# A two-layer decode kernel on one core: one transpose per K unit, a q projection with stationary weights, and a new plan of loads

## The chip, the cores and the metric

One core of a Trainium2 chip. The metric is device time in microseconds for one execution of the whole program; lower is better.

## The reference

Two rounds of attention and feed-forward with the same weights and the same K and V caches. Batch 4, one query token, 32 query heads over 8 K/V heads, 8192 cached positions, head size 128, model width 512, feed-forward width 1792, everything in bf16.

```python
def _A_ref(x, k_cache, v_cache, wq, wo):
    q = (x @ wq).reshape(B, Sq, Hq, Dh).transpose(0, 2, 1, 3)
    k = jnp.repeat(k_cache, rep, axis=1); v = jnp.repeat(v_cache, rep, axis=1)
    scores = jnp.einsum("bhqd,bhkd->bhqk", q, k) * (Dh ** -0.5)
    o = jnp.einsum("bhqk,bhkd->bhqd", _softmax(scores), v)
    return o.transpose(0, 2, 1, 3).reshape(B, Sq, Hq * Dh) @ wo

x = x + _A_ref(_layernorm(x), A_k_cache, A_v_cache, A_wq, A_wo)   # layer 0
x = x + _B_ref(_layernorm(x), B_w_gate, B_w_up, B_w_down)
x = x + _A_ref(_layernorm(x), A_k_cache, A_v_cache, A_wq, A_wo)   # layer 1, same caches
x = x + _B_ref(_layernorm(x), B_w_gate, B_w_up, B_w_down)
```

K and V are 64 one-MiB units each (named by batch, group of heads and half of the cache). Both layers read all of them; what stays in SBUF between the layers need not be read twice.

## The kernel before

All loads go through one queue, which before's profile shows busy for 97.7% of 16 DMA engines' time; a load counts as landed when its semaphore has been raised 16 times:

```python
def dma(self, engname, out_ap, in_ap, sem, reads=(), writes=()):
    self._wait(engname, self._need(reads, writes))
    ins = self.eng[engname].dma_start(out_ap, in_ap)
    ...
    ins.then_inc(sem, 16)
```

A scheduler in Python, with a planned duration for each step, fixes the order of work on each engine; `ORDER` fixes the order of the loads, and with it which units are kept. At run time each engine works strictly in that order: in after, TensorE waits 4.07 us for one unit while the next in its order has lain there since 620.64 us (shown below).

```python
ORDER = ("c320 K c321 ... b231 b350 b330 b331 b361 ")   # ... cut; K: the next K unit, a/b/c: V units, w: weights
NSLOT = 11
KM = (0, 0, 0, 0)            # K units kept of each batch
```

A K unit is transposed in place in two halves, and its scores are 32 matmuls of 512 columns (4 slices of the head x 4 blocks of rows x 2 halves), so that they need both halves early on:

```python
for h in range(2 if ld is not None else 0):
    def t(h=h):
        ap, key = unit_ap(u, h)
        v = ap.bitcast(mybir.dt.uint32)
        op("dve", lambda e: e.transpose(v, v), reads=[key], writes=[key])
    tr.append(PL.add("dve", 1.23, t, [ld], prio))
...
for es_ in range(NES):
    for a in range(4):
        for h in range(2):
            op("pe", lambda e: e.matmul(ps[...], lhsT=qpad[rows, qbuf, es_, g, :], rhs=ap[h][rows, :, es_ // 2, :, es_ % 2], ...))
```

Between the layers, batch by batch, lies what I call a crossing: the rest of layer 0 for that batch, the feed-forward block, and the q projection of layer 1, in two halves of 16 heads with the activations stationary and `wq` moving, which leaves the result in rows (128x512 in the trace) that VectorE transposes in 0.73 us:

```python
def q_rows(hf, deps, tag):
    ...
    for kt in range(KT):
        for n in range(4):
            op("pe", lambda e: e.matmul(ps[32 * n:32 * n + B, bk * BW:(bk + 1) * BW],
                                        lhsT=xnT[:, kt * B:(kt + 1) * B], rhs=w[:, :, 32 * n:32 * (n + 1)], ...))
```

Of the kernel before, what the change touches and what calls it, by code (L numbers as in the profile page):

```python
# [115 lines left out]
class Plan:  # L116
# [140 lines left out]
    def emit(self):  # L257
        for s in sorted(self.steps + self.loads, key=lambda s: (s.start, s.prio[0])):
            s.fn()


ORDER = ("c320 K c321 c041 c240 a061 wg0 K a071 c241 wo2 K x wq K c201 a051 a021 K c131 K c130 a031 c311 K K "
         "c110 K c111 K K c120 c121 c051 c040 K K K K K wo0 K a020 K a030 wg1 K a060 wo3 K c261 a070 K c050 K "
         "K K K c301 c260 K K K K K K a050 K a040 a041 a000 a001 wo1 a011 a010 c340 wd1 wu0 c341 wu1 wd0 a140 "
         "a141 a160 a171 a170 a161 K K K K K c200 K K K K K K c300 K K K K K a100 a101 a150 a151 K K a130 K "
         "a120 a121 K K K K K a111 K K K K K a110 K K a131 b000 b001 K b021 b030 b020 b070 b031 b071 b010 "
         "b011 K K K a210 K K K K K K K K K K K K K a270 a271 K a220 a250 a221 K a211 K K a230 a240 K K K "
         "b100 c060 K a200 a241 K c061 K a251 a231 K K K K a260 a201 a261 b150 K K b101 b161 b151 b170 b160 "
         "b171 b140 b141 K a310 a350 K K K K K K K K K K a351 K K K K K a370 a361 a360 a371 a330 a301 a340 "
         "a320 a341 a311 a300 a331 a321 b210 b211 b270 b271 b230 K K K K K K K K K K K K K K K K b221 b251 "  # L270
         "b250 b220 b371 b370 b351 b310 b360 b231 b350 b330 b331 b361 ")
NSLOT = 11
NP = 2
NQB = 1
LATE = (6, )
KM = (0, 0, 0, 0)
TAILSPLIT = True


def bass_interleave_layers__gqa_block_cached__swiglu_ffn__decode_kernel(  # L280
# [12 lines left out]
    B, _, D = A_x.shape  # L293
    _, G, S, Dh = A_k_cache.shape
# [19 lines left out]
    with ExitStack() as es:  # L314
# [107 lines left out]
        def pbk(key):  # L422
            return PL.bank[key]
# [46 lines left out]
                           reads=[f"wq{kt}", "xnT"], writes=[f"pb{bk}"], sig=(kt == KT - 1 and h == heads[-1]))  # L470
            return PL.add("pe", 0.029 * KT * len(heads), mm, deps, CHAIN, take=tag, n=2 * KT * len(heads))

        def q_rows(hf, deps, tag):
            nh = Hq // 2

            def mm():
                bk = pbk(tag)
                for kt in range(KT):
                    w = wq_sb[:, kt, hf * nh * Dh:(hf + 1) * nh * Dh].rearrange("p (h d) -> p h d", d=Dh)
                    for n in range(4):  # L480
                        op("pe", lambda e: e.matmul(ps[32 * n:32 * n + B, bk * BW:(bk + 1) * BW],  # L481
                                                    lhsT=xnT[:, kt * B:(kt + 1) * B],
                                                    rhs=w[:, :, 32 * n:32 * (n + 1)],
                                                    start=(kt == 0), stop=(kt == KT - 1), tile_position=(0, 32 * n)),
                           reads=[f"wq{kt}", "xnT"], writes=[f"pb{bk}"], sig=(kt == KT - 1 and n == 3))
            return PL.add("pe", 1.3, mm, deps, CHAIN, take=tag, n=2 * 4 * KT)

        def q_spread(src, n, key, deps, tag):
            def mm():
                bk = pbk(tag)  # L490
# [46 lines left out]
        def q_half(b, hf, mm_tag, deps, prior):  # L537
            nh = Hq // 2
            k = kpos[(1, b)] % NQB

            def scl():
                bk = pbk(mm_tag)
                blk = bank(bk).bitcast(mybir.dt.uint32)
                op("dve", lambda e: e.transpose(blk, blk), reads=[f"pb{bk}"], writes=[f"pb{bk}"])  # L544
                src = ps[:, bass.ds(bk * BW + b, nh, step=32)]
                op("dve", lambda e: e.tensor_scalar(qT2[:, hf * nh:(hf + 1) * nh], src, qscale[:, b:b + 1], None,  # L546
                                                    op0=ALU.mult),
                   reads=[f"pb{bk}", "qscale"], writes=[f"qT2_{hf}"])
            s1 = PL.add("dve", 0.98, scl, deps, CHAIN, free=mm_tag)
            tag = f"qs{b}_{hf}"  # L550
            sp = q_spread(qT2[:, hf * nh:(hf + 1) * nh], nh, f"qT2_{hf}", [s1], tag)

            def cp():
                bk = pbk(tag)
                got = ps[:, bk * BW:bk * BW + NES * nh].rearrange("p (s g j) -> p s g j", s=NES, j=REP)
                op("dve", lambda e: e.tensor_copy(q_diag(k, hf * G // 2, G // 2), got),
                   reads=[f"pb{bk}"], writes=[f"qpad{k}_{hf}"])
            return PL.add("dve", 0.21, cp, [sp, prior], CHAIN, free=tag)
# [36 lines left out]
        def k_pair(u, ld, prio, prev):  # L595
            _, l, b, g, cp = u
            qbuf = kpos[(l, b)] % NQB
            tr = []
            seq = [x[3:] for x in k_units(l, b)]
            first, last = [[c for c in seq if c[1] == cp][i] == (g, cp) for i in (0, -1)]  # L600
            for h in range(2 if ld is not None else 0):
                def t(h=h):
                    ap, key = unit_ap(u, h)
                    v = ap.bitcast(mybir.dt.uint32)
                    op("dve", lambda e: e.transpose(v, v), reads=[key], writes=[key])  # L605
                tr.append(PL.add("dve", 1.23, t, [ld], prio))
            qd = q_ready[(l, b)][2 * g // G]

            def qk():
                kt = [unit_ap(u, h) for h in range(2)]  # L610
                ap = [k[0].rearrange("p (t e j s) -> p t e j s", e=2, j=32, s=2) for k in kt]
                for es_ in range(NES):
                    for a in range(4):
                        rows = slice(32 * a, 32 * (a + 1))
                        for h in range(2):
                            c = 2 * cp + h
                            op("pe", lambda e: e.matmul(ps[32 * c:32 * (c + 1), a * BW:(a + 1) * BW],  # L617
                                                        lhsT=qpad[rows, qbuf, es_, g, :],
                                                        rhs=ap[h][rows, :, es_ // 2, :, es_ % 2],
                                                        start=(first and es_ == 0),  # L620
                                                        stop=(last and es_ == NES - 1),
                                                        tile_position=(32 * a, 32 * c), skip_group_check=True),
                               reads=[f"qpad{qbuf}_{2 * g // G}", kt[h][1]], writes=[f"pb{a}"],
                               sig=(es_ == NES - 1 and a == 3 and h == 1))
            st = PL.add("pe", 1.95, qk, tr + [qd, prev] + (scores_free[0] or []), prio, n=64)
            if u not in kept_k:
                st.slot_of = home[u]
            return st
# [249 lines left out]
        def chain(b, deps, prior):  # L878
# [6 lines left out]
            mm = None  # L885
            for hf in range(2):
                tag = f"q{b}_{hf}"
                mm = q_rows(hf, [cen, mm], tag)
                out_.append(q_half(b, hf, tag, [mm, qs], prior))
            if b == B - 1:  # L890
                mm.gives = KT
# [185 lines left out]
```

## Time and profile before

| | before |
|---|---|
| median of 4 runs | 640.68 us (639.79 to 641.46) |
| profiled span | 638.1 us |
| K and V loads | 231 of 1 MiB, 256.14 MB with the weights |
| one-MiB load in an undisturbed stretch | 2.487 us from landing to landing, 421 GB/s |
| last load landed | 627.12 us |

In the profile, the busy line, the queue's share and the chain that ended last say that transfers set the time; the prediction below shows them.

```profile
q8 instruction: 65, 1.06, 0.7%
...
L605 DVE STREAM_TRANSPOSE pool<-pool 128x1024 uint32<-128x1024 uint32 x240 | 284.2, 1222 | 72.8 <-DMA pool<-in_A_k_cache_dram 66.6
```

Columns of the first: packets, MB, share of 16 engines' time. 65 packets, each of 16,384 bytes in the trace; 8,273 matmuls and as many weight loads are 16,546 instructions, 255 to a packet. I read each as a page of TensorE's instructions. The second: 240 transposes of half a unit, mean 1222 ns.

The end of the stream in TensorE's timeline (start, duration, what, and in brackets the idle time before it and what ended it):

```profile
624.68 1.05 PE L758 MATMUL ps<-pool,pp 128*32 128x256 bf16 x16 [0.84 <-DMA pool<-in_A_v_cache_dram]
625.93 0.59 PE L743 MATMUL ps<-pp,pool 128*128 128x4 bf16 x16 [0.20 <-DMA pool<-in_A_v_cache_dram]
627.16 0.59 PE L743 MATMUL ps<-pp,pool 128*128 128x4 bf16 x16 [0.65 <-DMA pool<-in_A_v_cache_dram]
627.61 0.99 PE L721 MATMUL ps<-oT,wo_sb 128*128 128x4 bf16 x32
```

Each load is used the moment it lands, and 0.5 us after the last one the output projection starts.

### The profile page before, as it was taken

The numbers are of one execution on the slowest core, as the hardware profiler recorded it, in microseconds if no ns is written. First come the engines' busy times: TensorE is split into PE (matmuls) and PEld (weight loads), VectorE is DVE, ScalarE is ACT, GpSimd is POOL, SyncE is SP. The second block draws the span as 40 slices with busy tenths as digits, with TensorE's granted clock in tenths as the row PEclk, the third lists the DMA queues.
The fourth block names the chain that finished last, engine by engine and source line by source line (L and its number), as shares of the span: only waits on it lengthen the run. The fifth ranks groups of instructions, "written<-read, shape, count | busy, mean of one in ns | idle before, by whom it ended". The sixth has DMA issues, their size and how long they took to land.

```text
span 638.1 us, 17970 instructions
## 1 busy us (share of the span) xinstructions
PE 420.7 (66%) x8273; PEld 198.9 (31%) x8273; DVE 428.0 (67%) x752; ACT 40.2 (6%) x106; POOL 1.8 (0%) x8
## 2 busy tenths in 40 slices
PE   0176566756677776677677576768577766876576
PEld 0131133224332242135322232225332244522255
DVE  3248868863379886766689857467588762599632
ACT  0000100011000020000100100000200020000200
POOL 1000000000000000000000000000000000000000
PEclk9997668685556667676676777575766675578685
DMA  8999999999989999999999999999999999999992
GB/s 349 416 421 420 408 404 421 418 410 390 412 347 417 423 419 419 422 418 408 407 398 421 422 417 420 422 419 412 416 405 420 416 420 421 393 420 420 421 416 85
DMA packets 41124, 257.29 MB, mean 403 GB/s; under 512 B 3924, under 2 KB 9816, under 8 KB 11096
## 3 DMA queue, kind: packets, MB, share of 16 engines
q1 hardware_dynamic: 41048, 256.14, 97.7%
q8 instruction: 65, 1.06, 0.7%
q14 instruction: 11, 0.09, 0.0%
HBM read 256.12 MB, written 0.00 MB: 401 GB/s over the span
## 4 chain that ended last, share of the span: by engine, by line
DMA 66%; DVE 15%; PE 15%; SPq 2%; issue 2%; ACT 0%
DMA pool<-in_A_k_cache_dram 37%; DMA pool<-in_A_v_cache_dram 24%; DVE pool L605 10%; PE ps L617 5%; PE ps L758 4%; DMA wo_sb<-in_A_wo_dram 3%; DMA wq_sb<-in_A_k_cache_dram 2%; SPq L92 2%; PE ps L481 1%; PE ps L804 1%; DVE negm L636 1%; PE ps L676 1%; DVE ps L544 1%; DVE ps L785 1%; DVE wq_sb L605 1%
## 5 line engine op out<-in xcount | busy, mean ns | idle before, releaser
L605 DVE STREAM_TRANSPOSE pool<-pool 128x1024 uint32<-128x1024 uint32 x240 | 284.2, 1222 | 72.8 <-DMA pool<-in_A_k_cache_dram 66.6
L617 PE MATMUL ps<-pool,qpad 32*32 32x512 bf16 x3840 | 222.0, 542 | 75.7 <-DVE pool L605 75.1
L758 PE MATMUL ps<-pool,pp 128*32 128x256 bf16 x1952 | 99.8, 358 | 61.1 <-DMA pool<-in_A_v_cache_dram 44.9
L617 PEld LDWEIGHTS ps<-pool,qpad 32*32 32x32 bf16 x3840 | 63.9, 109 | 210.6 <-DVE pool L605 149.9
L758 PEld LDWEIGHTS ps<-pool,pp 128*32 128x32 bf16 x1952 | 56.1, 120 | 101.6 <-DMA pool<-in_A_v_cache_dram 62.6
L785 DVE STREAM_TRANSPOSE ps<-ps 128x256 f32<-128x256 f32 x63 | 28.8, 458 | 65.6 <-PE ps L758 65.6
L640 ACT ACTIVATE pp<-ps,negm 128x512 bf16<-128x512 f32 x32 | 21.5, 685 | 305.5 <-DVE negm L636 289.0
L721 PE MATMUL ps<-oT,wo_sb 128*128 128x4 bf16 x640 | 22.6, 166 | 15.5 <-DVE oT L789 7.5
L636 DVE TENSOR_REDUCE negm<-ps 128x1 f32<-128x512 f32 x32 | 19.9, 683 | 16.5 <-PE ps L617 16.5
L721 PEld LDWEIGHTS ps<-oT,wo_sb 128*128 128x128 bf16 x640 | 20.0, 102 | 27.3 <-DVE oT L789 13.6
L676 PE MATMUL ps<-ident,pp 128*128 128x128 bf16 x128 | 14.2, 285 | 9.1 <-DVE pp L665 8.3
L605 DVE STREAM_TRANSPOSE wq_sb<-wq_sb 128x1024 uint32<-128x1024 uint32 x16 | 18.6, 1212 | 0.5 <-DMA wq_sb<-in_A_k_cache_dram 0.2
L452 ACT ACTIVATE lnv<-var,eps_sb 128x4 f32<-128x4 f32 x10 | 3.0, 297 | 234.6 <-DVE var L447 234.6
L617 PE MATMUL ps<-wq_sb,qpad 32*32 32x512 bf16 x256 | 12.6, 409 | 7.1 <-DVE wq_sb L605 6.9
L676 PEld LDWEIGHTS ps<-ident,pp 128*128 128x128 bf16 x128 | 11.3, 131 | 15.9 <-DVE pp L665 11.0
L481 PE MATMUL ps<-wq_sb,xnT 128*4 128x512 bf16 x128 | 13.9, 589 | 1.9 <-DVE qT L546 1.4
L965 PE MATMUL ps<-ident,pp 4*128 4x4 bf16 x4 | 0.3, 167 | 21.0 <-DMA pp<-in_A_x_dram 21.0
L787 DVE TENSOR_REDUCE osum<-ps 128x4 f32<-128x32 f32 x63 | 12.1, 192 | 2.1
L789 DVE TENSOR_TENSOR oT<-osum,invL 128x4 bf16<-128x4 f32 x63 | 10.6, 169 | 2.1
L544 DVE STREAM_TRANSPOSE ps<-ps 128x512 uint32<-128x512 uint32 x8 | 5.8, 725 | 7.8 <-PE ps L481 7.8
L685 ACT ACTIVATE pp<-ps 128x1024 bf16<-128x1024 bf16 x8 | 8.2, 1023 | 35.3 <-PE ps L676 35.3
L804 PE MATMUL ps<-xnT,wu_sb 128*128 128x4 bf16 x280 | 8.6, 166 | 2.0 <-DVE gs L824 1.5
(69 smaller groups left out, 160.0 us busy)
## 6 DMA issues: line engine op xcount, KB each, us to landing
pool<-in_A_k_cache_dram SPq DMA_DIRECT2D x120, 1024.0 KB, 10.5
pool<-in_A_v_cache_dram SPq DMA_DIRECT2D x98, 1024.0 KB, 11.8
wq_sb<-in_A_k_cache_dram SPq DMA_DIRECT2D x8, 1024.0 KB, 14.4
wo_sb<-in_A_wo_dram SPq DMA_DIRECT2D x4, 1024.0 KB, 16.5
wq_sb<-in_A_wq_dram SPq DMA_DIRECT2D x1, 4096.0 KB, 18.5
wq_sb<-in_A_v_cache_dram SPq DMA_DIRECT2D x4, 1024.0 KB, 16.6
wg_sb<-in_B_w_gate_dram SPq DMA_DIRECT2D x2, 896.0 KB, 12.4
wd_sb<-in_B_w_down_dram SPq DMA_DIRECT2D x2, 896.0 KB, 13.1
```

The costliest lines, as they stand in the source:

```text
L92: ins = self.eng[engname].dma_start(out_ap, in_ap)
L481: op("pe", lambda e: e.matmul(ps[32 * n:32 * n + B, bk * BW:(bk + 1) * BW], lhsT=xnT[:, kt * B:(kt + 1) * B], rhs=w[:, :, 32 * n:32 * (n + ...
L544: op("dve", lambda e: e.transpose(blk, blk), reads=[f"pb{bk}"], writes=[f"pb{bk}"])
L605: op("dve", lambda e: e.transpose(v, v), reads=[key], writes=[key])
L617: op("pe", lambda e: e.matmul(ps[32 * c:32 * (c + 1), a * BW:(a + 1) * BW], lhsT=qpad[rows, qbuf, es_, g, :], rhs=ap[h][rows, :, es_ // 2, ...
L636: op("dve", lambda e: e.tensor_reduce(negm[:, q, a:a + 1], bank(a), AX.X, ALU.max, negate=True), reads=[f"pb{a}"], writes=[f"negm{q}_{a}"])
L640: op("act", lambda e: e.activation(pblk(q)[:, :, a, :], bank(a).rearrange("p (t j) -> p t j", j=32), ACTF.Exp, bias=negm[:, q, a:a + 1], s ...
L676: op("pe", lambda e: e.matmul(stg[:, t * P:(t + 1) * P], lhsT=pp[:, q, blk * P:(blk + 1) * P], rhs=ident[:], is_transpose=True, start=True ...
L721: op("pe", lambda e: e.matmul(ps[:, OPJ * BW + nq * B:OPJ * BW + (nq + 1) * B], lhsT=wo_sb[:, h, nq * P:(nq + 1) * P], rhs=oT[:, l, h, :], ...
L758: op("pe", lambda e: e.matmul(ps[32 * n:32 * (n + 1), bk * BW:bk * BW + 256], lhsT=pp[:, q, col:col + 32], rhs=v[:, 8 * f:8 * (f + 1), 32 ...
L785: op("dve", lambda e: e.transpose(blk, blk), reads=[f"pb{bk}"], writes=[f"pb{bk}"])
L804: op("pe", lambda e: e.matmul(ps[:, bk * BW + (fo - f0) * B:bk * BW + (fo - f0 + 1) * B], lhsT=w_sb[:, kt, fo * P:(fo + 1) * P], rhs=xnT[: ...
```

## The change

Its intent: fewer VectorE instructions (one transpose of 2048 elements per K unit in place of two of 1024), a shorter chain at the crossings (`wq` stationary, so that the result comes out in columns, 128x4 each, and the transposes of 0.73 us fall away), four K units of batch 0 kept, and an order of loads found anew for these durations.

```diff
-ORDER = ("c320 K c321 ... b231 b350 b330 b331 b361 ")
+ORDER = ("c100 c101 K K ... b311 b350 b331 b330 b361 ")      # all of it is new; cut
-KM = (0, 0, 0, 0)
+KM = (4, 0, 0, 0)
+MERGE = True
@@ the projection: q_rows goes, q_proj (used before for layer 0 alone) takes its place
-                mm = q_rows(hf, [cen, mm], tag)
+                mm = q_proj(range(hf * Hq // 2, (hf + 1) * Hq // 2), [cen, mm], tag)
@@ scaling of q
-                blk = bank(bk).bitcast(mybir.dt.uint32)
-                op("dve", lambda e: e.transpose(blk, blk), reads=[f"pb{bk}"], writes=[f"pb{bk}"])
-                src = ps[:, bass.ds(bk * BW + b, nh, step=32)]
+                src = ps[:, bass.ds(bk * BW + b + hf * nh * B, nh, step=B)]
...
-            s1 = PL.add("dve", 0.98, scl, deps, CHAIN, free=mm_tag)
+            s1 = PL.add("dve", 0.21, scl, deps, CHAIN, free=mm_tag)
@@ transposes of a K unit
-            for h in range(2 if ld is not None else 0):
-                ... (one half each)
-                tr.append(PL.add("dve", 1.23, t, [ld], prio))
+            def t(hs):
+                keys = [unit_ap(u, h)[1] for h in hs]
+                v = slot_sb(PL.slot[home[u]])[:, hs[0] * UE:(hs[-1] + 1) * UE].bitcast(mybir.dt.uint32)
+                op("dve", lambda e: e.transpose(v, v), reads=keys, writes=keys)
+            if ld is not None and MERGE:
+                tr.append(PL.add("dve", 2.27, lambda: t((0, 1)), [ld], prio))
+            ... (without MERGE: the two halves, as before)
```

## The prediction

> **What bounds the kernel now.** I began with the page's head: the transfers are busy nearly everywhere, the computing engines about two thirds.
>
> ```profile
> PE 420.7 (66%) x8273; PEld 198.9 (31%) x8273; DVE 428.0 (67%) x752; ACT 40.2 (6%) x106; POOL 1.8 (0%) x8
> ...
> q1 hardware_dynamic: 41048, 256.14, 97.7%
> ...
> DMA 66%; DVE 15%; PE 15%; SPq 2%; issue 2%; ACT 0%
> ```
>
> One queue moves 256.14 MB in a 638.1 us span, busy 97.7% of it, and two thirds of the chain that ended last is transfers. VectorE and TensorE are not bounds; they matter where they free one of the 11 one-MiB slots too late and the queue has nothing to fetch. So the next view is the table of stretches, cut where the GB/s dips (last column GB/s, before it the transfers' busy share):
>
> ```profile
> 138.00:164.00 26.00, 16.16 (x364) 12.08 (x348) 11.29 (x44) 4.86 (x13) 0.00 (x0) 0.57 1.04 396
> 173.00:183.00 10.00, 7.19 (x144) 3.68 (x144) 5.24 (x13) 0.00 (x0) 0.00 (x0) 0.50 0.72 283
> 183.00:296.00 113.00, 82.53 (x1576) 34.28 (x1561) 88.94 (x126) 4.86 (x13) 0.00 (x0) 0.67 1.01 420
> 304.00:330.00 26.00, 18.12 (x319) 8.57 (x311) 20.25 (x36) 3.99 (x10) 0.00 (x0) 0.70 0.97 396
> 440.00:476.00 36.00, 25.92 (x481) 13.76 (x488) 24.54 (x61) 4.49 (x12) 0.00 (x0) 0.64 1.00 408
> 548.00:564.00 16.00, 12.60 (x251) 5.92 (x251) 11.40 (x25) 0.50 (x2) 0.00 (x0) 0.61 0.99 392
> 627.20:638.10 10.90, 7.12 (x219) 6.54 (x219) 3.14 (x16) 0.75 (x3) 0.00 (x0) 0.50 0.02 3
> ```
>
> Undisturbed stretches give 420 GB/s, so 256.14 MB need 609.9 us, and the tail after the last landing takes 10.9. Against 420 the dips lose: 173 to 183: 10 x (420-283)/420 = 3.3 us; 304 to 330: 1.5; 440 to 476: 1.0; 548 to 564: 1.1; together 6.9. (138 to 164 loses 1.5 too, but at busy share 1.04: there the weights land; that is slow traffic, not an idle queue.) So 7 us, 1.1% of the span, is about all that removing waits can win.
>
> The largest dip is batch 0's crossing from layer 0 to layer 1 (timeline):
>
> ```profile
> 169.81 1.88 PE L481 MATMUL ps<-wq_sb,xnT 128*4 128x512 bf16 x16
> 171.74 0.73 DVE L544 STREAM_TRANSPOSE ps<-ps 128x512 uint32<-128x512 uint32 x1 [0.94 <-PE ps L481]
> 172.51 0.23 DVE L546 TENSOR_SCALAR qT<-ps,qscale 128x16 bf16<-128x16 f32 x1
> 172.79 1.88 PE L481 MATMUL ps<-wq_sb,xnT 128*4 128x512 bf16 x16 [1.11 <-DVE qT L546]
> 174.73 0.73 DVE L544 STREAM_TRANSPOSE ps<-ps 128x512 uint32<-128x512 uint32 x1 [1.99 <-PE ps L481]
> 175.49 0.23 DVE L546 TENSOR_SCALAR qT<-ps,qscale 128x16 bf16<-128x16 f32 x1
> ...
> 177.06 1.90 PE L758 MATMUL ps<-pool,pp 128*32 128x256 bf16 x32 [0.35 <-DVE qpad L556]
> ```
>
> No slot comes free from the V units that end at 167.7 until the first V unit behind the projection, near 178.0. The queue's own waits for 164 to 185 say the same; the longest is the 10 us one:
>
> ```profile
> SPq L62 <- PE ps L758: 22.0, 6, 10.0
> ```
>
> [...] the K transpose records 1222 ns (1189 at least), [...] this kernel's first projection did 128 of 4 columns in 3.57 us, 27.9 ns each, weight loads included. [...]
>
> **The change part by part.**
>
> Bytes. Four K units of batch 0 stay in their slots, minus 4 MiB. But the plan has 21 kept V units in place of 25 (43 second loads in place of 39), plus 4 MiB. The sum is zero: 256.14 MB again, as 218 + 12 + 1 one-MiB K and V loads before and the same 231 after. The 609.9 us stay.
>
> Merged transpose. [...] 2.27 us in place of two instructions that take 2.37 to 2.38 as a pair in the timeline (302.8 us busy for 256, 1.18 each). 124 units are transposed, not 128, and each saves 0.11. VectorE: 124 x 2.27 = 281.5 us, so 21 us less busy time: 9.5 from the kept units, 12 from merging. Nothing starts later by it: the score matmuls alternate between the halves, so the second already needed both. VectorE is not the bound; worth on the path is 0.1 us per K unit where a slot is awaited.
>
> Projection. Per half 16 matmuls of 512 columns (1.88 us at clock 0.5, 1.7 at the last crossing) become 64 of 4 columns: 64 x 27.9 ns = 1.79 us. Behind each, the 0.73 us PSUM transpose falls away. The order of instructions shows that the second half still waits once for VectorE, so batch 0's chain is 169.8 + 1.8 + 0.3 + 1.8 + 0.3 = 174.0 where scaling ended at 175.7 before: 1.7 us shorter. Four crossings, 8 transposes: 5.8 us off VectorE; TensorE unchanged within 1 us.
>
> New plan. At batch 0's crossing four K units now lie in their slots, transposed; the first score unit stands straight behind the projection. It needs 1.95 us before its slot is free, where the V unit before needed 0.95. First release: 178.0 - 1.7 + 1.0 = 177.3, about 0.7 us earlier. Counting the loads in the order of instructions, five units are outstanding at that point in both kernels (7 kept and 4 others now, 6 and 5 before), so the cover is equal, 5 x 2.5 us. The queue's dry time falls by 0.7, and perhaps 0.3 more as further kept units free slots without VectorE. From there both plans run on about five working slots and six kept.
>
> Sum on the path: crossing 0: -1.0; 304 to 330, where score units followed VectorE (5.6 us of TensorE waiting for the transposes) and the projection now runs unsplit: half of 1.5, -0.7; 548 to 564: half of 1.1, -0.5; 440 to 476: -0.4, since its dip at 468 to 472 again precedes a run of transposes. Total -2.6: 640.7 - 2.6 = 638.1. The halves are my choice: the new plan places other loads there.
>
> **The rivals.**
> - A wait in place of the one removed. A transpose of 2.3 us cannot be interrupted, so a scaling step behind it waits up to 1.1 us more; and until the first crossing four slots are tied up by K, which leaves seven or fewer for the rest. Against it: before, kept units also grew to six by then. If true: +1 to +3, 641 to 643.
> - All dips vanish: the plan was sought with better durations. Then -6.9 gives 634; for it, VectorE loses 27 us; against it, the dips follow softmax and chain lengths that stay.
> - The transfer is hidden anyway: dips move elsewhere in the same sum, and the time is 640 to 641. For it: the same bytes, the same 11 slots, and a schedule that was tuned before.
> - TensorE's instruction supply: 128 pairs in place of 32 per crossing behind the feed-forward block could stall. The first projection shows 27.9 ns over 128 pairs, so I give this 0.5 us per crossing at most.
>
> **Range and chances.** The prediction is 638.0. All dips gone is 634, no gain 640.7, a bad plan 643. I put 8 in 10 on 635.3 to 640.8. Over 2% faster needs 628, which is 609.9 + 10.9 + about 7 for start, slow weights and draining: no dips and more, 2%. Over 2% slower needs 653.5, 12.8 us more idle queue, 2%. Within 2%: 96%.
>
> **What would show it.** Right: transferred bytes at 256.1 MB and a share of 97.7 to 98.5%; a K transpose group of 124 with a mean of 2.25 to 2.3 us; VectorE busy near 400 us; no 128x512 PSUM transpose; the projection at about 3.6 us of TensorE per crossing; the dip at batch 0's crossing near 2.3 us of lost transfer, with the queue's longest wait there near 9 in place of 10; a tail of 10.9. Wrong: a new dip elsewhere over 1.5 us, which the table of stretches would show with a busy share under 0.95; projection pairs at 40 ns or more; or transposes of over 2.35 us.

2.27 us for a merged transpose, the 0.11 us saved by each and the 12 us of VectorE that follow stand as estimates; 2.27 us is also what the changed kernel plans for the step (2308 ns measured). Before's trace shows a K transpose of 1222 ns, and 128 matmuls of 4 columns in 3.57 us at a granted clock of 1.0, from which the 1.79 us are worked out. That parts are valued by transfer time rests on the queue's 97.7% and the chain's 66%. For "cannot be interrupted" the traces show this much: in after, 124 merged transposes took 2.27 to 2.32 us each, and none of VectorE's other records overlaps one by more than 0.09 us, at its ends.

## More of the kernel before

For V, a group's two units are used in a fixed order, each after the one before it (`prev`), whichever lands first; only the very last unit comes in two half loads:

```python
for i, cp in enumerate(VCP):
    ...
    st = PL.add("pe", ..., columns if direct else rows, [prev, p_ready[(l, b)], lds.get(u)], ...)
    prev = st
```

In before's trace each of the 231 K and V loads has 16 increments. I read them as one from each engine; the trace does not name the engine of an increment. TensorE starts on the last load at 627.16 us, 0.04 after its sixteenth increment (627.12).

## The result, and the profile after

| | before | after |
|---|---|---|
| median | 640.68 us (4 runs) | 640.39 us (639.93 to 641.15, 4 runs) |
| profiled span | 638.1 us | 637.9 us |
| last load landed | 627.12 us | 626.56 us |
| K and V loads | 231 | 231 |

The ratio of after to before is 0.9997, 95% interval 0.998 to 1.0014: the same. The value lies inside the predicted range, but the predicted gain of 2.7 us did not come: it is 0.3.

The lines of after that answer to those shown of before, first the page:

```profile
PE 401.5 (63%) x8657; PEld 202.0 (32%) x8657; DVE 405.2 (64%) x612; ACT 40.2 (6%) x106; POOL 1.8 (0%) x8
...
q1 hardware_dynamic: 41048, 256.14, 97.8%
q8 instruction: 67, 1.10, 0.7%
...
DMA 64%; PE 16%; DVE 13%; SPq 3%; issue 2%; ACT 0%
...
L589 DVE STREAM_TRANSPOSE pool<-pool 128x2048 uint32<-128x2048 uint32 x116 | 267.1, 2308 | 88.4 <-DMA pool<-in_A_k_cache_dram 87.9
...
L467 PE MATMUL ps<-xnT,wq_sb 128*128 128x4 bf16 x640 | 18.3, 166 | 12.8 <-DMA wq_sb<-in_A_wq_dram 11.5
```

VectorE fell from 428.0 to 405.2 us and has 140 instructions fewer, the bytes are the same, a merged transpose takes 2308 ns: all close to the forecast. TensorE has 384 matmuls more (8657 against 8273), each with its weight load (PEld has the same counts): 768 instructions, and two or three more pages. Then the crossing of batch 0, TensorE's timeline:

```profile
179.66 1.87 PE L467 MATMUL ps<-xnT,wq_sb 128*128 128x4 bf16 x64
181.86 1.87 PE L467 MATMUL ps<-xnT,wq_sb 128*128 128x4 bf16 x64 [0.33 <-DVE qT L530]
184.06 0.29 PE L480 MATMUL ps<-qT,ident 128*32 128x16 bf16 x16 [0.33 <-DVE qT L530]
...
184.91 1.05 PE L605 MATMUL ps<-pool,qpad 32*32 32x512 bf16 x16
```

From the start of the projection to the end of the second scaling (in VectorE's timeline) it is now 4.3 us (179.66 to 184.00) where it was 5.9 (169.81 to 175.72): 1.6 us shorter; 1.7 was forecast. And the stretches where the prediction saw dips (last columns the transfers' busy share and GB/s):

```profile
184.00:192.00 8.00, 7.20 (x168) 3.23 (x176) 3.59 (x7) 0.00 (x0) 0.00 (x0) 0.57 0.75 284
300.00:330.00 30.00, 19.47 (x446) 11.74 (x446) 18.53 (x33) 4.50 (x12) 0.00 (x0) 0.66 1.00 415
430.00:476.00 46.00, 29.91 (x680) 16.93 (x668) 30.01 (x62) 4.75 (x13) 0.00 (x0) 0.67 1.01 417
548.00:564.00 16.00, 12.63 (x350) 8.99 (x350) 10.94 (x22) 0.50 (x2) 0.00 (x0) 0.50 1.01 417
626.65:637.90 11.25, 7.67 (x236) 7.01 (x235) 3.96 (x19) 0.75 (x3) 0.00 (x0) 0.50 0.01 2
```

By the prediction's own measure the dips did shrink: 8 x (420-284)/420 = 2.6 us at the crossing (3.3 before), and 0.4, 0.3 and 0.1 for the next three (1.5, 1.0 and 1.1 before). In these stretches that is 3.5 us less, more than the 2.6 forecast, and yet the time is the same. Two cautions. A second execution of after (e9) shows 292, 402, 414 and 391 GB/s in the same four stretches, 5.5 us lost, so only 1.4 less than before; and the rate between the dips counts too, which the table below takes in. Even so, the measure is wrong, or the gain was given back. Both turned out true.

**Where it went, read from the landings.** The trace holds every semaphore increment, so for each load there are 16 landing times, by my reading one per DMA engine. I call the first of the 16 the fastest engine, the last the slowest. I summed, for the first of the 16, for their mean and for the last, how much later each load landed than 2.487 us per MiB after the load before it. This table is worked out from the increments, not a view of the profile (us lost in each stretch of time, and the landing of the last load):

```
run     engine     0-160  160-205  205-295  295-340  340-430  430-475  475-540  540-585  585-700    total   last
before  fastest     2.78     4.68    -0.19     2.90    -0.15     2.09     0.26     2.01    -0.06    14.31  624.54
before  mean        4.31     3.43     0.79     2.14     0.76     1.38     0.78     1.36     0.54    15.49  625.91
before  slowest     5.78     3.26     1.45     1.38     1.39     0.58     1.41     0.99     0.34    16.58  627.12
after   fastest     1.76     5.46     0.23     1.62     0.28     1.30     1.17     0.35    -0.04    12.13  622.00
after   mean        2.91     4.36     0.85     1.29     1.00     1.15     1.12     0.64     0.33    13.65  623.93
after   slowest     4.44     3.99     1.26     0.83     1.51     0.16     1.44     1.42     0.84    15.90  626.56
a second execution of after (run e9 below):
after   fastest     1.56     5.25     0.40     1.97    -0.13     1.74     0.58     1.89    -0.07    13.19  623.44
after   mean        2.90     4.18     0.89     2.11     0.69     1.12     0.72     1.50     0.37    14.47  624.84
after   slowest     4.57     3.76     1.35     1.08     1.61     0.72     1.47     1.44    -0.01    16.00  626.55
```

In the first execution the fastest engine is done 2.54 us earlier, which is the forecast, and the mean of them 1.98 (in the second 1.10 and 1.07). The slowest gains only 0.56 and 0.57, and a load counts as landed only with the slowest (the 627.16 after 627.12 above). The 16 increments are not in step: at the end of before the last of them lags the first by 2.6 us, in after by 4.6, in e13 by 5.3, one to two whole loads of 2.487 us. Run e13 below, which does the same work in the same order up to the last loads, is a third execution: 2.05 earlier for the fastest engine, 1.11 for the mean, and 0.66 later for the slowest. So the slowest engine's gain is not resolved from zero, and it is below the mean's in all three. At 295 to 340 us of before, the fastest lost 2.90 and the slowest 1.38. My reading: in a dip the fast engines have run out of work while the slowest is still busy with older loads.

**Why one engine lags.** Where the slowest landing falls behind in one step, while the fastest loses nothing, an instruction page had just been fetched, and it was every eighth one. After, each step of the slowest landing of 0.9 us or more after the first weights, with the page before it:

```
after: landing  step   page (number, time)
        31.38  +1.13    #1   28.33
       110.70  +1.11    #9  108.03
       193.21  +1.84   #17  187.92   (also the crossing's dip: the fastest engine lost 4.06)
       266.72  +0.98   #25  264.36
       335.21  +0.98   #33  330.98
       413.66  +1.00   #41  410.68
       484.58  +0.99   #49  481.91
       555.56  +0.95   #57  553.21
       624.07  +0.94   #65  619.87   (the last loads)
```

A page is one packet of 1.07 us in the trace (median of 65 records in before and of 68 in after). The trace does not name the engine of a page, but the period of eight suggests that pages go to eight engines in turn, and the 16 landings of one load agree. Of the load that landed at 624.07, behind #65, one engine was last, seven were 0.96 to 1.40 us earlier and eight 3.57 to 4.56. That fits eight engines without pages, seven with eight pages each, and one with a ninth. Before shows the same steps (39.52 +1.28 after #1, 116.53 +1.49 after #9, 186.86 +1.41 after #16, 265.29 +1.35 after #24, 412.40 +0.80 after #39, 485.87 +0.77 after #47, 559.37 +0.78 after #55); at 559.37 the fastest engine lost 0.99 too. From #9 to #16 and from #24 to #39 the distance is one short of a multiple of eight, so the slowest engine was not the same one throughout. The next of the last class, #63, came at 625.87, too late to delay the last loads by the full step.

**The tail.** From the last landing to the end of the profiled span it was 11.0 us and is now 11.3. TensorE's timeline of after:

```profile
624.11 1.05 PE L746 MATMUL ps<-wq_sb,pp 128*32 128x256 bf16 x16 [4.07 <-DMA wq_sb<-in_A_v_cache_dram]
625.09 0.59 PE L709 MATMUL ps<-oT,wo_sb 128*128 128x4 bf16 x16
625.61 1.04 PE L746 MATMUL ps<-pool,pp 128*32 128x256 bf16 x16
626.59 1.01 PE L731 MATMUL ps<-pp,pool 128*128 128x4 bf16 x32
627.65 1.01 PE L709 MATMUL ps<-oT,wo_sb 128*128 128x4 bf16 x32
```

TensorE waits 4.07 us for the unit that landed at 624.07 and takes it first; the unit it takes at 625.61 had landed at 620.64. The new plan loads the two in the reverse of the order of use (`b331 b330` where before had `b330 b331`). So 1 us of work that could have been done in the wait stands between the last landing and the projection, which starts at 627.65 where it started at 627.61. So all of the 0.56 us was given back here. The span is 0.26 us shorter only behind the last computation: the output's store is issued at 636.23 (before 636.18) and done sooner.

The theory that I took to the chip: (T) the end is set by the slowest DMA engine, which carries every eighth instruction page at about 1 us each (1.07 us a page, steps of 0.94 to 1.13 above, 1.84 in the dip), so what the change took out of the dips was time in which that engine was not idle; the small rest was lost in the tail. The main rival (P) is the prediction's own view, in which the mean rate counts and pages are hidden.

### The profile page after: what moved, and what is told of

The parts are those of the page before. It is cut to its first block, busy times and chain, and to the rows that moved or that the text cites. A ratio compares the mean times of both kernels' runs of the same rounds, so it can differ in the third digit from the quotient of the medians. Undisturbed runs are those within 1.5% of the kernel's fastest.

```text
span 637.9 us, 18599 instructions
## 1 busy us (share of the span) xinstructions
PE 401.5 (63%) x8657; PEld 202.0 (32%) x8657; DVE 405.2 (64%) x612; ACT 40.2 (6%) x106; POOL 1.8 (0%) x8
## 3 DMA queue, kind: packets, MB, share of 16 engines
q1 hardware_dynamic: 41048, 256.14, 97.8%
## 4 chain that ended last, share of the span: by engine, by line
DMA 64%; PE 16%; DVE 13%; SPq 3%; issue 2%; ACT 0%
DMA pool<-in_A_k_cache_dram 45%; DMA pool<-in_A_v_cache_dram 12%; DVE pool L589 9%; PE ps L605 8%; DMA wq_sb<-in_A_k_cache_dram 5%; PE ps L746 4%; SPq L92 3%; DMA wq_sb<-in_A_v_cache_dram 3%; PE ps L467 1%; DVE negm L624 1%; DVE wq_sb L589 1%; PE ps L792 1%; PE ps L664 1%; PE ps L845 1%; DVE ps L773 1%
## 5 line engine op out<-in xcount | busy, mean ns | idle before, releaser
L589 DVE STREAM_TRANSPOSE pool<-pool 128x2048 uint32<-128x2048 uint32 x116 | 267.1, 2308 | 88.4 <-DMA pool<-in_A_k_cache_dram 87.9
L605 PE MATMUL ps<-pool,qpad 32*32 32x512 bf16 x3840 | 197.4, 548 | 130.8 <-DVE pool L589 125.6
L605 PEld LDWEIGHTS ps<-pool,qpad 32*32 32x32 bf16 x3840 | 55.5, 110 | 248.4 <-DVE pool L589 185.8
L709 PE MATMUL ps<-oT,wo_sb 128*128 128x4 bf16 x640 | 22.4, 166 | 11.3 <-DVE oT L777 8.4
L467 PE MATMUL ps<-xnT,wq_sb 128*128 128x4 bf16 x640 | 18.3, 166 | 12.8 <-DMA wq_sb<-in_A_wq_dram 11.5
L467 PEld LDWEIGHTS ps<-xnT,wq_sb 128*128 128x128 bf16 x640 | 17.7, 104 | 15.3 <-DMA wq_sb<-in_A_wq_dram 11.6
L589 DVE STREAM_TRANSPOSE wq_sb<-wq_sb 128x2048 uint32<-128x2048 uint32 x8 | 18.5, 2312 | 1.8 <-DMA wq_sb<-in_A_k_cache_dram 1.8
L673 ACT ACTIVATE pp<-ps 128x1024 bf16<-128x1024 bf16 x8 | 8.2, 1024 | 30.1 <-PE ps L664 30.1
L845 PE MATMUL ps<-hT,wd_sb 128*128 128x4 bf16 x280 | 8.6, 166 | 1.8 <-issue 1.1
L653 DVE TENSOR_SCALAR pp<-pp,alpha 128x512 bf16<-128x512 bf16 x32 | 9.0, 344 | 1.1 <-ACT alpha L646 1.1
```

The lines of the kernel that those rows point to most:

```text
L467: op("pe", lambda e: e.matmul(ps[:, bk * BW + h * B:bk * BW + (h + 1) * B], lhsT=wq_sb[:, kt, h * Dh:(h + 1) * Dh], rhs=xnT[:, kt * B:(kt ...
L589: op("dve", lambda e: e.transpose(v, v), reads=keys, writes=keys)
L605: op("pe", lambda e: e.matmul(ps[32 * c:32 * (c + 1), a * BW:(a + 1) * BW], lhsT=qpad[rows, qbuf, es_, g, :], rhs=ap[h][rows, :, es_ // 2, ...
L709: op("pe", lambda e: e.matmul(ps[:, OPJ * BW + nq * B:OPJ * BW + (nq + 1) * B], lhsT=wo_sb[:, h, nq * P:(nq + 1) * P], rhs=oT[:, l, h, :], ...
L845: op("pe", lambda e: e.matmul(ps[:, bk * BW + nq * B:bk * BW + (nq + 1) * B], lhsT=wd_sb[:, fo, nq * P:(nq + 1) * P], rhs=hT[:, fo * B:(fo ...
```

## The experiments

All runs were correct unless I say so. Each row's ratio is to the kernel before on the same chip. "Slowest" is the slowest engine's last landing in the profiled execution (627.12 before, 626.56 after), to be read with care: one execution each, and between after and e13, which differ in the last loads alone, it moved by 1.2 us.

| run | median us | ratio, 95% | pages | slowest |
|---|---|---|---|---|
| e1 merge alone | 643.48 | 1.0051, 1.0035 to 1.0066 | 65 | 631.22 |
| e2 projection alone | 641.77 | 1.0023, 1.0005 to 1.0041 | 67 | 628.96 |
| e3 plan alone | 647.37 | 1.0108, 1.0087 to 1.0130 | 65 | 634.03 |
| e16 merge and projection | 647.86 | 1.0118, 1.0103 to 1.0133 | 68 | 635.58 |
| e8 merge and plan | 641.28 | 1.0009, 0.9987 to 1.0030 | 65 | 627.65 |
| e7 projection and plan | 647.09 | 1.0098, 1.0073 to 1.0122 | 68 | 632.57 |
| e9 all (after again) | 640.33 | 0.9991, 0.9971 to 1.0012 | 67 | 626.55 |
| e4 after, projection at crossing 0 only | 640.71 | 1.0008, 0.9993 to 1.0023 | 65 | 627.56 |
| e10 after, at crossings 0 and 2 | 642.24 | 1.0019, 0.9998 to 1.0040 | 66 | 629.45 |
| e11 after, at 0, 2 and 3 | 642.29 | 1.0017, 0.9998 to 1.0036 | 67 | 628.54 |
| e5 after, 16 small matmuls per unit | 669.70 | 1.0438, 1.0408 to 1.0469 | 99 | 653.61 |
| e6 after, 4 wide matmuls per unit | 654.01 | 1.0208, 1.0174 to 1.0242 | 75 | 642.99 |
| e12 after, thinned (wrong result) | 633.16 | 0.9878, 0.9856 to 0.9900 | 36 | 620.61 |
| e15 thinned, 16 small ones (wrong result) | 640.45 | 1.0002, 0.9987 to 1.0016 | 67 | 626.48 |
| e13 after, last two loads swapped | 640.60 | 1.0008, 0.9993 to 1.0023 | 68 | 627.78 |
| e14 before, last two loads reversed | 640.56 | 1.0005, 0.9991 to 1.0019 | 65 | 627.02 |

### The parts alone (e1, e2, e3, e16, e7, e8)

e1 is before with `t((0, 1))` and one step of 2.27 us in place of two. e2 is before with `q_proj` and the scaling without transpose. e3 is before with

```diff
-ORDER = ("c320 K ...")   KM = (0, 0, 0, 0)
+ORDER = ("c100 c101 ...")   KM = (4, 0, 0, 0)
```

> The kernel before with one thing changed: one VectorE transpose per K unit. Theory T (the end is set by the slowest of the 16 DMA engines, which loses about 1 us for every eighth page of TensorE instructions): no matmul is added or removed, so as many pages as before (65), and VectorE's 12 us saved are slack: ratio to before 0.999 to 1.001 (640.1 to 641.3 us). Theory P (the prediction's: what counts is the mean rate of the stream in its dips): 0 to -0.5 us, since the queue waits for TensorE's release, which a merged transpose moves by 0.1 us at most. Rival R1 (a 2.3 us transpose that nothing can interrupt delays urgent VectorE work): +1 to +3 us.

Measured 643.48, +3.3 us. Neither T nor P had that; R1 had about the size. But where most was lost, at 295 to 340 us, no urgent step waited behind a long transpose at crossing 1: VectorE's first one there starts at 315.58. Elsewhere R1 was not looked for. The planned duration changed, the scheduler laid the work in another order, and each engine is bound to it. One place where the two differ: in before, the V unit between the two halves of crossing 1's projection ran without a wait at 303.45; here it was put before a load that had not come:

```profile
303.03 1.04 PE L762 MATMUL ps<-pool,pp 128*32 128x256 bf16 x16 [1.03 <-DMA pool<-in_A_v_cache_dram]
```

At 295 to 340 us the slowest engine lost 4.43 us here and 1.38 in before. That this one wait is the reason is not shown.

> The kernel before with the new q projection alone (plan, transposes and kept units as before). Theory P: the chain of the first crossing is 1.7 us shorter, so -0.7 to -1.0 us (639.7 to 640.0). Theory T: the crossing's loss on the slowest engine falls by 0.3 to 0.5 us, but 768 more TensorE instructions are 3 more pages, and the eighth page that in the kernel before came at 625.87 us, just behind the last loads, comes some 20 us earlier, onto the same engine as they: +0.9 us. Sum +0.3 to +0.6 us, 641.0 to 641.3. The landings by engine should show 9 steps of about +1 us against 8 in before.

Measured +0.23% with an interval from 0.05 to 0.41, that is +1.5 us (0.3 to 2.6): slower, as T said and P did not, but by more than T's 0.3 to 0.6, which only the low end of the interval reaches. The crossing's loss on the slowest engine fell from 3.26 to 2.68, about as T had it, but more was lost later: 2.43 against 1.41 at 475 to 540. The landings do not show T's nine even steps either. So the direction agrees with T, the size and the detail do not.

> The kernel before with the new plan of loads and kept units alone (old projection, two transposes per K unit). Theory P: its dips of 1.5, 1.0 and 1.1 us are the ones that the plan removed, worth the prediction's -0.7 -0.5 -0.4 = -1.6 us: 639.1. Theory T: in those dips the slowest engine lost only 0.3 to 0.7 us of which the pages alone are most, and there are 65 pages as before, so the one page that hits the last loads in the changed kernel does not come: -0.3 to -0.9 us against before, 639.8 to 640.4, and faster than the changed kernel by 0 to 0.6 us. Rival R2 (the old transposes and the old chain don't fit the plan made for the new): over +1 us.

Measured +1.1%, 6.7 to 7.3 us more than before: R2, and neither P nor T. The new plan with the old durations runs into real stalls (4.28 us lost on the slowest engine at 430 to 475).

So none of the three parts is a gain by itself. Three more runs complete the table of all combinations. e16 is before with the edits of e1 and e2:

> The kernel before with merged transposes and the new projection on the old plan. If the plan is fitted to the other two (merged transposes alone +3.3 us, projection alone +1.5, plan alone +7): +2 to +6 us against before. If the two changes need each other and not the plan: 0.

Measured +1.2%: fitted to the plan. e7 is after with

```diff
-MERGE = True
+MERGE = False
```

> The changed kernel with the two 1.22 us transposes per K unit again, new plan and projection kept. With the merged transpose costing the old plan +3.3 us and the new plan alone costing +7, the question is which of the two the new plan needs. If the new plan is fitted to the merged transpose (its step for it is 2.27 us, so loads are released in other places): +4 to +7 us against the changed kernel, with dips of both the fastest and the slowest DMA engine after 295 us as in the run with the plan alone. If it is the projection that the plan needs: within 1 us of the changed kernel.

Measured 647.09, the first case. e8 is after with the old projection at all crossings:

> The changed kernel with the old projection at all four crossings, merged transpose and new plan kept (768 TensorE instructions, 3 pages fewer). Prediction's own figures: the first crossing's chain is 1.7 us longer again, +0.7 to +1.0 us. Theory T: that loss at the first crossing, less 0.4 us for 3 pages fewer; 0 to +1 us against the changed kernel. If the plan needs the projection at the later crossings, as the run with it at the first crossing alone hints (1.7 us of loss on the slowest engine came back at 430 to 475 us): +2 to +3 us.

Measured 1.0009 against after's 0.9997 and 0.9991, 0.9 us by the medians and within the noise of these runs: the small values of the expectation, which the prediction's figure and T share, so this run does not tell them apart. Together: on the new plan the merged transpose is worth about 1% (e7 against after), on the old plan it costs 0.5%; the projection makes no difference that can be resolved on the new plan. In these runs a plan of loads is good only with the durations that it was made for, and the change's three parts mostly repay each other.

### After again, and the projection at some crossings (e9, e4, e10, e11)

> The changed kernel itself, unaltered, on the same chip as the three runs beside it, to compare them with: ratio to before 0.998 to 1.001; the landing of the slowest DMA engine in its last load about 0.6 us earlier than before, that of the fastest about 2.5 us earlier.

The slowest engine's last landing was 626.55 (626.56 in the first profile), while the fastest engine's was 623.44 against 622.00. The expectation for the fastest (2.5 us earlier than before) missed: 1.1. What the fast engines gain varies between executions; what the slowest gains is the same 0.56 both times. The step at the last loads was not there in this execution (-0.01 us at 585 to 700): the slowest engine had lost its time earlier. So page #65 at the last loads is one way to that landing, not its cause.

The other three keep `q_rows` at some crossings, for fewer instructions:

```diff
+STAT = (0, )          # e4; (0, 2) in e10, (0, 2, 3) in e11
-            mm = q_proj(...)
+            mm = q_proj(...) if b in STAT else q_rows(hf, [cen, mm], tag)
```

> The changed kernel with wq stationary only in the crossing to the first batch, and the old projection in the other three (576 fewer TensorE instructions, 2.25 pages). Theory T: the page that came at 619.87 us onto the slowest engine comes over 20 us later, after the last load: -0.7 to -0.9 us against the changed kernel, 639.5 to 639.8, and -0.9 to -1.2 us against before. Theory P: the later crossings showed no dip of over 1 us in the kernel after, and their chain is 1.7 us longer again: 0 to +0.5 us against the changed kernel.

> The changed kernel with wq stationary in the crossings to batches 0 and 2, the old projection at 1 and 3. In the run with it at batch 0 alone the stage of crossing 1 lost 0.7 us less on the slowest engine than in the changed kernel, and the stage of crossing 2 lost 1.7 us more. If the two are independent: -0.7 us against the changed kernel (639.7), with 1.5 pages fewer. If the stages depend on each other through the plan: 0 to +1 us.

> The changed kernel with the old projection at crossing 1 alone, where the new one showed a wait of 1.91 us for instructions. Independent stages: -0.7 us against the changed kernel, the wait of 1.91 us gone. Otherwise 0 to +1 us.

In e9 the ratio and the slowest engine's 0.57 us came as expected; the fastest engine's 2.5 us did not come again (1.10). The other three missed what T hoped for. e4 is 0.1% above after's own ratios, inside the noise. e10 and e11 are 1.9 and 2.0 us slower than e9 by the medians, in the same rounds on the same chip; of their twelve runs only one (640.97) is below e9's slowest (641.06). So both are worse than even the second case of their expectations. The wait of 1.91 us is gone in e11, with one of 1.03 us for VectorE in its place. With 65 pages, e4 still had steps near the end (+1.05 at 546.65 and +1.11 at 617.77 us): taking away two pages moves the pages, and does not keep the last ones off the slowest engine. And the stages depend on each other: 430 to 475 us lost 1.89, 2.39 and 2.19 us on the slowest engine in the three, 0.16 and 0.72 in the two executions of after. All three have the old projection at crossing 1 (near 300 us), and lose more at crossing 2 (near 445): how one crossing is done seems to change what is ready at the next.

### More instructions (e5, e6)

Matmuls with zero weights, accumulated ahead of the last matmul of each K and V unit:

```diff
+        def pad(rows, out, rhs, at, key, src):
+            for i in range(PAD):     # e5: 16 of 4 columns; e6: 4 of 256 columns
+                op("pe", lambda e: e.matmul(out, lhsT=zt[rows, :], rhs=rhs, start=False, stop=False, ...),
+                   reads=["zt", src], writes=[key], sig=False)
```

> The changed kernel plus 16 matmuls of 4 columns with zero weights in every K unit and nearly every V unit (results unchanged; some 3,950 instructions, 15 pages more; at 28 ns each some 0.45 us of TensorE work per unit). Theory T: 15 more pages are some 2 more on each of the 8 DMA engines that carry them, the slowest one too: +2.0 us against the changed kernel from pages, plus what the longer TensorE work costs, which the next run measures alone. Theory P, and the view that instruction pages are spread thin and hidden: no more than the next run.

> Control of the run before: 4 matmuls of 256 columns with zero weights per unit in place of 16 of 4 columns, so at least as much TensorE time [...], but only 990 instructions, 4 pages. Theory T: +0.5 us from pages plus the cost of the TensorE time; the run with 16 small ones should be slower than this one by 1 to 1.5 us less whatever the wider ones' extra time costs. The view that TensorE's time alone counts: this one is the slower of the two.

(Measured, the padding itself kept TensorE busy for 149.1 us in e5 and 192.5 in e6, summed over its groups.)

Measured 669.7 and 654.0. TensorE's busy time is nearly equal (495.2 and 488.4 us), and the run with more instructions is 15.7 us slower, so the view that only TensorE's time counts falls. But T's size falls too: 1 to 1.5 us was expected. I had also counted half of the instructions, since each matmul comes with a weight load: 99 pages against 75 and 67. Even so 24 pages are 3 on each of T's eight engines. The views of TensorE's waits name the rest (us in total, times, longest; the first three of e5, the last of e6):

```profile
PE ps L400 <- issue: 21.3, 11, 3.3
PE ps L762 <- issue: 12.8, 10, 2.7
PE ps L618 <- issue: 10.2, 10, 2.3
```

```profile
PE ps L618 <- issue: 2.1, 2, 1.3
```

"Issue" is time in which TensorE waited for nothing that the profile shows. In e5 it is 44 us over these three lines, up to 3.3 at a time. The profile does not call it waiting for instructions, but the pages' times do: of the 33 waits for "issue" of over 0.5 us in e5, 32 end 1.2 to 1.6 us after a page has landed, a window in which a moment taken at random falls 7% of the time; so do all three of after. So, by my reading, a crowd of small instructions costs twice here: TensorE waits for them (the 44 us), and their pages hold up a DMA engine (steps of 4.5 us in e12 to e15, below). How the 15.7 us divide between the two is not measured; T had left the first out.

### The pages by themselves (e12, e15)

To see the pages without a late TensorE, e12 leaves out most of TensorE's work:

```diff
-                for es_ in range(NES):
+                for es_ in (NES - 1, ):          # scores: a quarter of the matmuls
...
-                        for f in range(2):
+                        for f in (1, ):          # values: half of them
...                                               # and the start flags to match
```

> The changed kernel with three quarters of the score matmuls and half of the value matmuls left out (result wrong on purpose): some 8,160 TensorE instructions fewer, 36 pages in place of 67, the same loads. Theory T (every eighth page costs the slowest DMA engine 1 us): 4 steps of about 1 us in its landings in place of 8 or 9, -4 us at the last landing from that; with what is left of dips, stream end at 619 to 622.5 us against 626.6, and a gap between the fastest and the slowest engine at the end of about half of 4.6 us. Rival (the dips alone cost, pages are hidden): with TensorE no longer late, the slowest engine's dips of 3.5 us go, stream end not before 622.5, the gap between the engines as before or larger.

and e15 adds 16 small matmuls per unit to it, as e5 did to after:

> The thinned kernel of the run before (result wrong on purpose, 36 pages, 5 steps of 1.5 us) plus 16 matmuls of 4 columns with zero weights per K and V unit: some 68 pages again, but TensorE busy for 350 us at most, so not late. Theory T (pages by themselves delay the slowest DMA engine): 8 to 9 steps again, +4 to +6 us at the slowest engine's last landing (620.6 to about 625 or 626), and the same in the time. Rival (only TensorE's time and its wait for instructions cost): 0 to +1 us.

TensorE's busy time and the pages, e12 and then e15:

```profile
PE 237.6 (38%) x4577; PEld 125.2 (20%) x4577; DVE 405.1 (64%) x612; ACT 40.2 (6%) x106; POOL 1.8 (0%) x8
...
q8 instruction: 36, 0.59, 0.4%
```

```profile
PE 389.0 (61%) x8641; PEld 259.1 (41%) x8641; DVE 405.0 (63%) x612; ACT 40.2 (6%) x106; POOL 1.9 (0%) x9
...
q8 instruction: 67, 1.10, 0.7%
```

and their steps, worked out from the increments as above:

```
e12: landing  step   page              e15: landing  step   page
      31.59  +1.43    #1   28.26             31.61  +1.46    #1   28.32
     186.32  +1.45    #9  183.66            125.63  +1.42    #9  123.29
     326.94  +1.54   #17  322.71            195.43  +1.48   #17  192.91
     477.53  +1.55   #25  474.23            276.43  +1.47   #25  274.11
     610.70  +1.55   #33  607.08            347.42  +1.49   #33  344.48
                                            425.93  +1.40   #41  422.68
                                            496.87  +1.24   #49  493.00
                                            560.44  +1.25   #57  555.97
                                            626.48  +0.82   #65  624.17
```

Pages #1, #9, #17 and so on, in each case, and no other step of this size. Five steps became nine, and the slowest engine's last landing went from 620.61 to 626.48, 5.9 us: T's 4 to 6, where the rival had 0 to 1. The steps add up to 7.5 us in e12 and 12.0 in e15, so they make 4.5 of the 5.9. The time rose by 7.3 us (633.16 to 640.45), more than T had for it. The 1.4 us beyond the stream are TensorE's: it waited 1.40 us for "issue" among the last small matmuls, until 626.72 (page #65 had landed 1.5 us before), and the output projection started 1.9 us after the last landing, where it was 0.5 in e12. T missed one more thing in e12: the gap between the fastest and the slowest engine did not halve, it was 5.1 us. My reading, which no run shows by itself: with fewer dips the fast engines wait less for the slow one, so that the gap says how far they ran ahead, not how late the slowest is.

Between the two runs TensorE's load rose as well as the pages, and its waits for "issue" rose from 1.7 to 15.0 us in total; the fastest engine's last landing moved by 8.4 us (615.50 to 623.92), so dips came back as well. The times alone would therefore prove little; the steps carry the argument: where the slowest engine lost a step while the fastest lost nothing (at most 0.1 us in all but the eighth step of e15), a queue without work for all 16 is not the reason. That e15 has the same last landing as after (626.48 and 626.56) with the same 67 pages agrees, but is one execution of each, and e13 with 68 landed at 627.78.

### The tail (e13, e14)

```diff
-  "... b351 b311 b350 b331 b330 b361 "      # e13, from after; e14 is the reverse edit in before
+  "... b351 b311 b350 b330 b331 b361 "
```

> The changed kernel with two loads of the plan swapped: the value unit that TensorE uses first now comes first (TensorE's order of work stays). Theory T2 (the stream's gain was given back in the tail, by TensorE waiting 4 us for the unit landing at 624.07 with the one landed at 620.64 still to do): the unit of 1 us leaves the end of the chain, so the output projection starts at about 627.1 in place of 627.65: -0.55 us against the changed kernel, profiled span 637.3 to 637.5, median 639.7 to 639.9, ratio to before about 0.998 to 0.9985. Rival (the end hangs on the last landing alone): no difference.

> The kernel before with the same two value units in the reversed (the changed plan's) order of loading. Theory T2: TensorE waits until 624.65 for the unit it uses first, then has two units and the last halves: 624.65 + 1.0 + 1.0 + 0.5, so that the projection starts at about 627.65 or, with the last half landing at 627.12 as before, a little later than 627.61: +0.0 to +0.5 us (here the last half lands so late that it hides most of it). Rival: no difference. This is a weak test, told as such.

TensorE's timeline of e13, then of e14:

```profile
626.58 0.59 PE L731 MATMUL ps<-pp,pool 128*128 128x4 bf16 x16 [0.20 <-DMA pool<-in_A_v_cache_dram]
627.83 0.58 PE L731 MATMUL ps<-pp,pool 128*128 128x4 bf16 x16 [0.66 <-DMA pool<-in_A_v_cache_dram]
```

```profile
624.67 1.04 PE L758 MATMUL ps<-pool,pp 128*32 128x256 bf16 x16 [3.17 <-DMA pool<-in_A_v_cache_dram]
...
627.14 1.01 PE L743 MATMUL ps<-pp,pool 128*128 128x4 bf16 x32
628.21 0.94 PE L721 MATMUL ps<-oT,wo_sb 128*128 128x4 bf16 x29
```

The mechanism is as described: in e13 the projection starts 0.5 us after the last landing (628.27 after 627.78), in e14 1.2 us (628.21 after 627.02), where before had 0.5 and after 1.1. The order of the last two loads is worth 0.6 to 0.7 us, in both directions. The time of e13 did not follow, though: in its profile the slowest engine fell behind after each of nine eighth pages, by +1.25 to +1.5 (+3.17 in the crossing's dip), the last time (622.83, +1.28) in the final loads, and landed 1.2 us later than in after. The gain of 0.55 us in time that I expected is therefore not shown: the interval, 0.9993 to 1.0023, lies above the expected 0.998 to 0.9985. e14's +0.05% agrees with the +0.6 us of its span (638.7 against 638.1) but isn't resolved either.

No version with a correct result beat both kernels.

## Why the prediction was wrong

- **Bytes, transposes, VectorE, projection.** Right or nearly: 256.14 MB, 2308 ns against 2.27 us (just over its 2.25 to 2.3), 405.2 us against "near 400" (22.8 off VectorE, where it had 27), and 1.87 us per half against 1.79. The prediction counted 124 transposes and the profile has 116 + 8. The 2.27 us were the estimate; measured, 1024 more elements in one instruction took 1086 ns (2308 against 1222), 136 less than as an instruction of their own.
- **Crossing 0, -1.0.** The chain became 1.6 us shorter (1.7 forecast). For the mean of the engines the stream up to 205 us lost 7.27 us where it had lost 7.74, -0.5 (-0.7 in e9, -0.3 in e13): about half of the step. I count from the start since the last weights land at 147 to 162 us in before and at 153 to 172 in after; the stream was slower around them (396 GB/s at 138 to 164 in before, against 420).
- **The three later dips, -0.7, -0.5 and -0.4.** (In the order 304 to 330, 548 to 564, 440 to 476.) For the mean engine -0.9, -0.7 and -0.2 in the first profile of after, 0.0, +0.1 and -0.3 in e9, and -1.0, -0.8 and -0.1 in e13, where 0.9 us was lost anew at 205 to 295. So they came about in two executions of three, and what the mean kept over the whole stream is 1.98, 1.07 and 1.11 us of the 2.6.
- **The step that failed** is the rule under all of these, "against 420 the dips lose: 10 x (420-283)/420 = 3.3 us ... together 6.9", which prices a dip by the mean GB/s, and so by the average engine (whose last landing moved by 1.98 us of the 2.6 in the first execution). A load counts as landed with the slowest of the 16, which fell behind by about 1 us with each eighth page and was still working in the dips. Its last landing moved by -0.56 and -0.57 us in the two profiles of after and by +0.66 in e13, less than the mean's in each.
- **"A tail of 10.9".** Mis-sized by 0.4: it is 11.3 from the last landing to the end. The new plan loads the last two units in the reverse of the order of use, which costs 0.6 to 0.7 (e13, e14) and cancels the 0.56; the spans differ by 0.26 for the output's store alone, and the medians by 0.3, within their scatter.
- **The rivals.** "The transfer is hidden anyway, 640 to 641" was the one that came true, in part for another reason: the gap was there to be filled, but not on the engine that counts. "TensorE's instruction supply, at most 0.5 us per crossing" was under-weighted: after shows 1.91 us of "issue" at crossing 1 and 0.95 at crossing 3, each ending 1.2 to 1.6 us after a page had landed, and the 768 extra instructions are also transfers (67 pages against 65).
- The number itself lay within the stated range because that range reached to "no gain"; the mechanism forecast a gain that the time does not show.
- What stays open: why e1 and e2 lose where they do, which of the many changes of order does it, and why executions of one kernel differ in which engine is the slowest (steps of 1.25 to 1.5 us in e13, of 0.9 to 1.1 in the first profile of after, hardly any even steps in e9).

## What to carry to other kernels

When a load lands by 16 increments, as here, price a gap in the stream by the last of them, not by the mean rate: look at all 16 increments of each load (here 2.54 us gained on the first and 0.56 on the last). TensorE's instructions came as transfers too, 1.07 us a page, so in a kernel bound by transfers try few wide matmuls in place of many small ones even where TensorE has time left: 31 pages more went with a last landing 5.9 us later (e12 to e15), and the run with small ones was 15.7 us slower than the one with wide ones (e5, e6). And when a tuned order of loads is changed, check at the end of the stream that units are loaded in the order in which they are used, and test the parts alone before crediting any of them: here each part alone was a loss, the merge too, 3.3 us (e1), which saves 0.1 us per unit by the prediction's estimate.
